# Element work of an attention-and-FFN kernel laid out anew over VectorE, ScalarE and GpSimd

## The chip, the cores and the metric

The kernel runs on one core of one Trainium2 chip. The metric is the device time of one execution in microseconds (us); lower is better. In this document PE is TensorE (matrix multiplies), DVE is VectorE, ACT is ScalarE, POOL is GpSimd and SP is SyncE, which here only starts transfers. PEld is PE's weight load. SBUF is the core's working memory and PSUM the memory that PE writes its results to. All times that are compared come from runs in the same, fast state, with a granted TensorE clock of 0.98 to 1.00.

## The reference, cut to what matters

Four batches, four heads and 1088 tokens of 32 values go through an attention without softmax, and its output (4352 tokens of 128 values) through a feed-forward network (FFN) with 2048 hidden values.

```python
def phi(x):                       # two sketches of 8 values, and all 64 products of them
    a = einsum('rd,bhsd->bhsr', S1, x)
    b = einsum('rd,bhsd->bhsr', S2, x)
    return einsum('bhsi,bhsj->bhsij', a, b).reshape(..., 64)
q_p, k_p = phi(q), phi(k)
kv  = einsum('bhsf,bhsd->bhfd', k_p, v)
z   = sum(k_p, axis=2)
num = einsum('bhsf,bhfd->bhsd', q_p, kv)
den = einsum('bhsf,bhf->bhs',  q_p, z)[..., None] + 1e-06
x   = (num / den)                 # then as 4352 x 128
h   = maximum(x @ w_in, 0)
out = (h * h) @ w_out
```

## The kernel before

The FFN is the spine of the program. Its tokens are cut into 12 chunks: each batch has two of 384 tokens and one of 320. A chunk takes 16 steps, one for each 128 hidden values. A step is one fp16 matmul (`pg`, the first FFN layer), a relu from PSUM to SBUF (`gt`), a square (`g2`), and one fp32 matmul (`po`, the second layer), which the trace records as two instructions. That makes 192 steps, and the attention of later chunks is slipped in between them, because it would otherwise leave PE idle.

A small planner puts every attention task at a step. It looks for the first step after the task's inputs at which its engine has room:

```python
class _Plan:
    LAG = {"PE": 2, "DVE": 1, "ACT": 1, "POOL": 1, "SP": 1}
    def add(self, key, eng, dur, needs, f, *args, not_in=(), first=0, lag=None):
        s = first
        for k in needs:
            s = max(s, self.at[k] + (self.LAG[eng] if lag is None else lag))
        while s < self.n - 1 and (
            (self.load[eng][s] > 0 and self.load[eng][s] + dur > self.cap[eng]) or ...):
            s += 1
        self.fix(key, eng, dur, s, f, *args)
...
P = _Plan(NS + 4, {"PE": 0.95, "DVE": 1.2, "ACT": 0.6, "POOL": 5.0, "SP": 9.0})
```

The k work of a batch n (once per batch, for batches 1 to 3) is planned in this order, and the last chunk of the batch before it was planned ahead of all of it:

```python
def k_tasks(n):
    for g in range(2):
        P.add(("fs", n, g), "DVE", 0.45, [("kf", n)], a_fs, n, g)
    P.at["X"] = P.at["fs", n, 1]
    P.add(("qT", n), "DVE", 1.25, [("fs", n, 0)], a_qT, n, 0, S)      # q of the whole batch
    P.add(("qg", n, 0), "PE", 0.5, ["X", ("qT", n)], a_qg, n, 0)
    for g in range(2):
        P.add(("kp", n, g), "DVE", 1.36, [("fs", n, g)], a_kp2, n, g)  # the 64 products of k
    P.add(("ks1", n), "DVE", 1.15, [("kp", n, 1)], a_ks1, n)           # sums of kp, for z
    P.add(("ks2", n), "DVE", 1.0, [("ks1", n)], a_ks2, n)
    P.add(("kv", n), "PE", 1.4, [("ks2", n), "N"], a_kv9, n)
    ...
```

"N" and "X" stand for two PSUM tiles that tasks share, and so for when they come free. The x work of a chunk divides numerator by denominator and scales the result by a power of two, so that it fits fp16:

```python
def a_rd(b, ch):
    ...
    nc.vector.tensor_scalar(out=de[:, 0:m], in0=_ap(st[b, "dT", ch], 0, 128, 0, [[32, m]]),
                            scalar1=1e-6, scalar2=None, op0=add)       # SBUF to SBUF, 12 values
    nc.vector.reciprocal(rd[:, 0:m], de[:, 0:m])
...
def a_qpn(b, ch, s):                                                   # the 64 products of q
    nc.vector.tensor_tensor(out=qp..., in0=st[b, "sh", ch, s, 0]..., in1=st[b, "sh", ch, s, 1]..., op=mult)
def a_s2(b, ch):                                                       # sm is in PSUM
    nc.vector.tensor_scalar(out=s2..., in0=st[b, "sm", ch]..., scalar1=EXP, scalar2=None, op0=band)
def a_rs(b, ch):                                                       # s2 is in SBUF
    nc.vector.tensor_scalar(out=rs..., in0=st[b, "s2", ch]..., scalar1=EXP, scalar2=None, op0=bxor)
def a_xs(b, ch):
    nc.vector.tensor_tensor(out=st[b, "xT"]..., in0=st[b, "x", ch]..., in1=st[b, "rs", ch]..., op=mult)
def a_beta(b, ch):                                                     # same tile twice
    nc.gpsimd.tensor_tensor(out=bt..., in0=st[b, "s2", ch]..., in1=st[b, "s2", ch]..., op=mult)
```

The relu of every step is on ACT. The square goes to ACT or DVE by a rule that looks at the planned attention work of this step alone, and remembers nothing of the steps before:

```python
def ffn1(i, sq_on_act, cols=None):
    ...
    nc.scalar.activation(gt[:, c0:c1], pg[:, c0:c1], Relu)
    if sq_on_act:
        nc.scalar.activation(g2[:, c0:c1], gt[:, c0:c1], Square)
    else:
        nc.vector.tensor_tensor(out=g2[:, c0:c1], in0=gt[:, c0:c1], in1=gt[:, c0:c1], op=mult)
...
def act_square(i):
    s = max(i - LA, 0)
    return P.load["ACT"][s] + 0.47 + 0.41 < P.load["DVE"][s] + 0.46
```

## Time and profile before

| before | value | from |
|---|---|---|
| time | 203.65 us, median of 3 runs (203.53 to 204.09) | the timed runs |
| span of the profiled run | 201.6 us | the page |
| PE busy | 192.5 us, 95% | the page |
| undisturbed step of 384 tokens, of 320 | 0.807 us, 0.674 us | starts of `pg` in the timeline |
| PE stretching, step 4 to the end of chunk 10 | 8.8 us | worked out, see below |

The page's first part gives busy time, share of the span and number of instructions of each engine. The second line below is its part on the chain of work that ended last, by engine.

```profile
PE 192.5 (95%) x1639; PEld 113.2 (56%) x1639; DVE 159.1 (79%) x369; ACT 149.1 (74%) x346; POOL 24.8 (12%) x86
...
PE 67%; DVE 16%; ACT 10%; issue 3%; DVEq 0%; ACTq 0%
```

PE looks full, at 95%, but a quarter of the chain runs through DVE and ACT. Both are true at once: a matmul that waits for its operand while another is in flight counts as busy. So the busy share does not tell what can be won. I therefore took the starts of successive `pg` matmuls, and compared each step's period with a floor: the period of those steps that hold the same PE matmuls and wait for nothing. Such periods repeat within about 0.01 us. The floor is 0.807 us (or 0.674 us), plus the attention matmuls in the step, above all 0.58 us for `qg` (the sketches of q), 1.29 for `ndn` (numerator and denominator) with `kf` (the sketches of k), about 1.2 for `ndn` with `qg`, 0.14 for `sm` (the sum behind the scale). At a change of chunk the two layers work on different widths, and the floor is 0.781 or 0.701 us. The excess, summed over steps 4 to 175, that is to the end of chunk 10, is 163.9 - 155.1 = 8.8 us. I call it PE stretching. The first four steps, which take 2.55 us in before, are left out.

The groups by form (line, engine, operation, out<-in, partitions x elements, count | busy us, mean ns | idle before, and what ended it) tell who does the element work of before:

```profile
L687 ACT ACTIVATE gt<-pg 128x384 f32<-128x384 f32 x127 | 60.5, 481 | 17.8 <-PE pg L678 16.0 <-DVE g L691 1.1
L691 DVE TENSOR_TENSOR g<-gt 128x384 f32<-128x384 f32 x55 | 30.1, 557 | 18.1 <-ACT gt L687 17.7
L521 DVE TENSOR_TENSOR xT<-x,rs 128x384 f16<-128x384 f32 x6 | 6.4, 1062 | 0.2
L434 DVE TENSOR_TENSOR qp<-sh 128x384 f32<-128x384 f32 x12 | 6.6, 548 | 0.2
L339 DVE TENSOR_TENSOR ks<-kp 128x1024 f32<-128x1024 f32 x3 | 3.7, 1224 | 0.1
```

Two products of the same size, `xT` and `qp`, take 1062 and 548 ns: `xT` runs while POOL computes `bt`, `qp` does not.

The stretching has two forms. The first is in this piece of the timeline of ACT and PE (start us, duration us, engine, line, operation). Relu and square of successive steps are both on ACT, 0.47 and 0.53 us, and `pg` starts every 0.93 us instead of 0.81:

```profile
66.77 0.53 ACT L689 ACTIVATE g<-gt 128x384 f32<-128x384 f32 x1
66.79 0.32 PE L678 MATMUL pg<-xT,w_in 128*128 128x384 f16 x1
67.20 0.47 ACT L687 ACTIVATE gt<-pg 128x384 f32<-128x384 f32 x1
67.70 0.52 ACT L689 ACTIVATE g<-gt 128x384 f32<-128x384 f32 x1
67.72 0.32 PE L678 MATMUL pg<-xT,w_in 128*128 128x384 f16 x1
```

The second form is DVE late around the k work. This is the timeline of DVE in batch 2's k work, with two lines of PE's:

```profile
79.72 1.27 DVE L252 STREAM_TRANSPOSE qT<-qn 128x1088 f32<-128x1088 f32 x1
80.91 1.31 DVE L284 TENSOR_TENSOR kp<-fs 128x1152 f32<-128x1152 f32 x1
81.13 0.56 PE L416 MATMUL qg<-qT,sqn 64*32 64x192 f32 x16 [0.26 <-DVE qT L252]
86.65 1.23 DVE L339 TENSOR_TENSOR ks<-kp 128x1024 f32<-128x1024 f32 x1
87.91 1.15 DVE L350 TENSOR_TENSOR ks<-ks 128x512 f32<-128x512 f32 x2
89.12 0.32 PE L327 MATMUL kvp<-ks,ones 128*32 128x64 f32 x8
```

PE waits for `qT` before it can do `qg`, and a step's square that DVE should do sits behind each of these instructions of 1.2 us and more, which are longer than a whole step.

### The profile page before, as it was taken

What the parts mean: (1) busy time and instruction counts of PE and PEld (TensorE: products, weight loads), DVE (VectorE), ACT (ScalarE), POOL (GpSimd) and SP (SyncE); (2) the same over time, 40 slices, a digit from 0 to 9 for tenths busy, and PEclk for the clock granted to TensorE, in tenths of its full rate; (3) what the DMA queues carried; (4) which work ended last, traced back from release to release, by engine and by line L of the source; (5) the groups of instructions that cost most, each with busy time, mean ns of one, the idle gap of its engine ahead of it and who ended that gap; (6) DMA issues with size and microseconds to landing.
All of it is one profiled execution on the core that took longest, in us unless ns stands there. A gap on an engine that the chain in (4) does not pass through costs nothing.

```text
span 201.6 us, 4402 instructions
## 1 busy us (share of the span) xinstructions
PE 192.5 (95%) x1639; PEld 113.2 (56%) x1639; DVE 159.1 (79%) x369; ACT 149.1 (74%) x346; POOL 24.8 (12%) x86
## 2 busy tenths in 40 slices
PE   7998999999999999999999999999999999999990
PEld 2963755446656455465545555455646555555890
DVE  3866975997888877998899777998799876676750
ACT  3456977997698968975969976976777987766730
POOL 4835132100010100100011000100010110000000
PEclk9999999999999999999999999999999999999997
DMA  6799410200284110020056220020020020010201
GB/s 190 192 312 255 139 23 0 42 0 3 34 208 133 16 16 3 2 42 2 0 126 169 81 32 3 0 42 0 2 44 0 0 36 0 14 25 0 39 3 33
DMA packets 27199, 11.40 MB, mean 57 GB/s; under 512 B 19178, under 2 KB 25770, under 8 KB 27178
## 3 DMA queue, kind: packets, MB, share of 16 engines
q1 hardware_dynamic: 26726, 11.02, 22.4%
q8 instruction: 13, 0.21, 0.5%
q10 hardware_dynamic: 452, 0.10, 0.2%
q14 instruction: 8, 0.07, 0.1%
HBM read 8.78 MB, written 2.23 MB: 55 GB/s over the span
## 4 chain that ended last, share of the span: by engine, by line
PE 67%; DVE 16%; ACT 10%; issue 3%; DVEq 0%; ACTq 0%
PE po L701 38%; PE pg L678 13%; ACT gt L687 6%; PE ndn L447 4%; ACT g L689 3%; DVE sh L425 3%; DVE kp L284 2%; PE warm L822 2%; PE pt L718 2%; DVE xT L521 1%; PE kvp L313 1%; DVE ks L339 1%; PE rep L839 1%; DVE ks L350 1%; PE qg L416 1%
## 5 line engine op out<-in xcount | busy, mean ns | idle before, releaser
L701 PE MATMUL po<-g,w_o 128*128 128x384 f32 (+3 forms) x386 | 144.1, 458 | 0.0
L687 ACT ACTIVATE gt<-pg 128x384 f32<-128x384 f32 (+2 forms) x193 | 87.9, 461 | 30.3 <-PE pg L678 28.4
L701 PEld LDWEIGHTS po<-g,w_o 128*128 128x128 f32 x386 | 66.1, 190 | 37.5 <-issue 26.3
L678 PE MATMUL pg<-xT,w_in 128*128 128x384 f16 (+2 forms) x193 | 61.0, 316 | 1.1 <-ACT gt L687 0.4
L689 ACT ACTIVATE g<-gt 128x384 f32<-128x384 f32 (+1 forms) x114 | 57.4, 504 | 3.6
L691 DVE TENSOR_TENSOR g<-gt 128x384 f32<-128x384 f32 (+2 forms) x79 | 41.3, 534 | 22.4 <-ACT gt L687 21.8
L678 PEld LDWEIGHTS <-w_in 128*128 128x128 f16 x193 | 18.8, 97 | 24.7 <-issue 7.1
L530 POOL TENSOR_TENSOR bt<-s 128x384 f32<-128x384 f32 (+1 forms) x10 | 9.2, 916 | 125.4 <-DVE s L503 125.4
L425 DVE STREAM_SHUFFLE sh<-qg 128x384 f32<-128x384 f32 (+1 forms) x40 | 20.7, 560 | 0.0
L434 DVE TENSOR_TENSOR qp<-sh 128x384 f32<-128x384 f32 (+1 forms) x20 | 10.4, 522 | 0.3
L521 DVE TENSOR_TENSOR xT<-x,rs 128x384 f16<-128x384 f32 (+1 forms) x10 | 9.9, 993 | 0.3
L447 PE MATMUL ndn<-qp,kw 64*32 64x192 f32 (+1 forms) x320 | 9.4, 318 | 0.6 <-DVE qp L434 0.6
L733 POOL COPY br<-beta 32x3 f32<-32x3 f32 x32 | 7.1, 222 | 12.5 <-DVE beta L641 11.3
L447 PEld LDWEIGHTS ndn<-qp,kw 64*32 64x32 f32 x320 | 5.0, 106 | 6.3 <-issue 2.9
L284 DVE TENSOR_TENSOR kp<-fs 128x1152 f32<-128x1152 f32 x6 | 7.9, 1325 | 0.0
L457 DVE STREAM_TRANSPOSE dT<-ndn 128x384 f32<-128x384 f32 (+1 forms) x10 | 5.5, 554 | 2.0 <-PE ndn L447 2.0
L747 DVE SCALAR_TENSOR_TENSOR sc<-po,bt 128x384 f32<-128x384 f32 (+1 forms) x9 | 4.8, 531 | 2.0 <-PE po L701 1.9
L313 PE MATMUL kvp<-kp,vn 128*32 128x64 f32 (+1 forms) x288 | 6.3, 222 | 0.0
L416 PE MATMUL qg<-qT,sqn 64*32 64x192 f32 (+1 forms) x160 | 5.8, 316 | 0.5 <-DVE qT L252 0.5
L313 PEld LDWEIGHTS kvp<-kp,vn 128*32 128x32 f32 (+1 forms) x288 | 4.9, 109 | 2.2 <-issue 1.1
L822 PE MATMUL warm<-zero 128*128 128x512 f16 x13 | 4.8, 529 | 1.2 <-DVE zero L149 1.2
L492 ACT ACTIVATE ax<-x,tiny 128x384 bf16<-128x384 f32 (+1 forms) x10 | 5.8, 579 | 0.0
(115 smaller groups left out, 136.8 us busy)
## 6 DMA issues: line engine op xcount, KB each, us to landing
vn<-in_v_dram SPq DMA_DIRECT2D x32, 64.0 KB, 3.5
kn<-in_k_dram SPq DMA_DIRECT2D x3, 544.0 KB, 11.1
qn<-in_q_dram SPq DMA_DIRECT2D x3, 544.0 KB, 4.1
out_dram<-oT SPq DMA_DIRECT2D x24, 48.0 KB, 1.8
w_in<-in_moe_w_in_dram SPq DMA_DIRECT2D x2, 512.0 KB, 5.3
w_o<-in_moe_w_out_dram SPq DMA_DIRECT2D x2, 512.0 KB, 10.1
out_dram<-oT SPq DMA_DIRECT2D x12, 40.0 KB, 2.5
out_dram<-ob SPq DMA_DIRECT2D x8, 48.0 KB, 1.8
```

Of the source, the lines that this page charges most:

```text
L284: nc.vector.tensor_tensor(out=_ap(st[b, "kp2"], 0, 128, 128 * NT * g, [[64, 2 * NT], [8, 8], [1, 8]]), in0=_ap(fs, 0, 128, 0, [[16, 2 * NT ...
L313: nc.tensor.matmul(st[b, "kvp"][32 * h : 32 * h + 32, 0:64], _ap(vn[b], 0, n, v0 + dv * h, [[1, 32]]), kp[0:n, at[h] : at[h] + 64], start= ...
L425: nc.vector.stream_shuffle(in_=_ap(st[b, "qg", ch], 0, 128, 0, [[512, 2], [1, n]]), out=_ap(t_, 0, 128, 0, [[n, 2], [1, n]]), mask=mask_q[ ...
L434: nc.vector.tensor_tensor(out=qp[:, 0 : 2 * n], in0=st[b, "sh", ch, s, 0][:, 0 : 2 * n], in1=st[b, "sh", ch, s, 1][:, 0 : 2 * n], op=mult,)
L447: nc.tensor.matmul(nd[32 * h : 32 * h + 32, 512 * g + 192 * i : 512 * g + 192 * i + n], st[b, "kw"][64 * g : 64 * g + 64, 128 * i + 32 * h ...
L521: nc.vector.tensor_tensor(out=st[b, "xT"][:, 384 * ch : 384 * ch + n], in0=st[b, "x", ch][:, 0:n], in1=st[b, "rs", ch][:, 0:n], op=mult,)
L530: nc.gpsimd.tensor_tensor(out=bt[:, 0:n], in0=st[b, "s2", ch][:, 0:n], in1=st[b, "s2", ch][:, 0:n], op=mult)
L678: nc.tensor.matmul(pg[:, c0:c1], w_in[:, 128 * c : 128 * c + 128], st[b, "xT"][:, 384 * ch + c0 : 384 * ch + c1],)
L687: nc.scalar.activation(gt[:, c0:c1], pg[:, c0:c1], Relu)
L689: nc.scalar.activation(g2[:, c0:c1], gt[:, c0:c1], Square)
L691: nc.vector.tensor_tensor(out=g2[:, c0:c1], in0=gt[:, c0:c1], in1=gt[:, c0:c1], op=mult)
L701: nc.tensor.matmul(st["po", b, ch][:, c0:c1], w_o[:, 128 * c : 128 * c + 128], g2s[i][1][:, c0:c1], start=first, stop=(c == NFF - 1), skip ...
```

## The change

The change wants to use POOL, busy for only 12%, and to take load from DVE:

1. Products whose operands are both in SBUF go from DVE to POOL: `qp`, `xT`, one of the two `kp` of a batch, and the sums `ks`.
2. `rs` is read from PSUM instead of from `s2` in SBUF, so that this DVE instruction reads no SBUF.
3. The relu of a step may be on DVE, and a square on POOL. A planner, `balance`, chooses for each step, and carries each engine's backlog from step to step.
4. The order in which tasks are planned changes: `kp` ahead of `qT`, `qT` in three pieces, the x work of the last chunk behind the next batch's k work, loads eight steps earlier, output work a step later. POOL's task durations are given as 0.95 to 2.7 us, and PE's are shortened.
5. The last of the nine token tiles of k has only 64 tokens. Its matmuls with v in `kv` now run over 128 rows for batches 1 to 3, and POOL sets the rows of v behind the tokens to zero.

```diff
     def a_kp2(b, g):
-        nc.vector.tensor_tensor(
+        (nc.vector if g == 0 else nc.gpsimd).tensor_tensor(
...
     def a_kv(b, t):                     # t counts the token tiles of k
-        n, v0, dv = (128, 512 * (t // 4) + 32 * (t % 4), 128) if t < 8 else (64, 1024, 32)
+        n = 64 if b == 0 and t == 8 else 128
+        v0, dv = (512 * (t // 4) + 32 * (t % 4), 128) if t < 8 else (1024, 32)
...
     def a_ks1(b):                       # ks2, qpn and xs likewise
-        nc.vector.tensor_tensor(
+        nc.gpsimd.tensor_tensor(
...
     def a_rs(b, ch):
-            out=rs[:, 0:n].bitcast(U32), in0=st[b, "s2", ch][:, 0:n].bitcast(U32),
-            scalar1=EXP, scalar2=None, op0=bxor,
+            out=rs[:, 0:n].bitcast(U32), in0=st[b, "sm", ch][:, 0:n].bitcast(U32),
+            scalar1=EXP, scalar2=EXP, op0=band, op1=bxor,
...
     def ffn1(i, on, cols=None):
-        nc.scalar.activation(gt[:, c0:c1], pg[:, c0:c1], Relu)
-        if sq_on_act:
+        if on[0] == "ACT":
+            nc.scalar.activation(gt[:, c0:c1], pg[:, c0:c1], Relu)
+        else:
+            nc.vector.tensor_scalar(out=gt[:, c0:c1], in0=pg[:, c0:c1], scalar1=0.0, ..., op0=amax)
+        if on[1] == "ACT":
             nc.scalar.activation(g2[:, c0:c1], gt[:, c0:c1], Square)
         else:
-            nc.vector.tensor_tensor(
+            (nc.vector if on[1] == "DVE" else nc.gpsimd).tensor_tensor(
...
-            P.fix(("ob", b, ch), "DVE", 0.56, s0 + 1, f_ob, b, ch)
+            P.fix(("ob", b, ch), "DVE", 0.56, s0 + 2, f_ob, b, ch)
...
     def loads(n):
+        nc.gpsimd.memset(vn[n][64:128, 1024:1152], 0.0)
...
     def k_tasks(n):
-        P.add(("qT", n), "DVE", 1.25, [("fs", n, 0)], a_qT, n, 0, S)
-        P.add(("qg", n, 0), "PE", 0.5, ["X", ("qT", n)], a_qg, n, 0)
         for g in range(2):
-            P.add(("kp", n, g), "DVE", 1.36, [("fs", n, g)], a_kp2, n, g)
+            P.add(("kp", n, g), ("DVE", "POOL")[g], (1.36, 2.7)[g], [("fs", n, g)], a_kp2, n, g)
+        turn_q(n, 0)
+        P.add(("qg", n, 0), "PE", 0.5, ["X", ("qT", n, 0)], a_qg, n, 0)
...
-        P.fix(("ld", n), "SP", 0.0, s0, loads, n)
+        P.fix(("ld", n), "SP", 0.0, max(s0 - 8, 0), loads, n)
...
-    x_tasks(0, 2)
     for n in range(1, B):
         k_tasks(n)
+        x_tasks(n - 1, 2)
+        kv_tasks(n)
         for ch in range(3):
             feature_tasks(n, ch)
-            if ch == 2 and n + 1 < B:
+            if ch < 2:
+                turn_q(n, ch + 1)
+            elif n + 1 < B:
                 turn_k(n + 1)
             nd_tasks(n, ch)
-            x_tasks(n, ch)
+            if ch < 2:
+                x_tasks(n, ch)
+                P.cap["DVE"] = CAP            # 0.99
+    x_tasks(B - 1, 2)
...
-    def act_square(i): ...
+    def balance():
+        load = {e: P.load[e] + [0.0] * 4 for e in ("PE", "ACT", "DVE", "POOL")}
+        late = {e: 0.0 for e in ("ACT", "DVE", "POOL")}
+        for s_ in range(NS - LA):
+            ...
+            for r, q_ in (("ACT", "ACT"), ("DVE", "ACT"), ("ACT", "DVE"), ("ACT", "POOL")):
+                own_ = {e: load[e][s_] for e in late}
+                own_[r] += cost[r]
+                own_[q_] += cost[q_]
+                if q_ == "POOL" and (late[q_] + own_[q_] > 1.0 or end_ >= -1):
+                    continue
+                end = {e: late[e] + own_[e] + 0.3 * load[e][s_ + 1] for e in late}
+                c_ = max(end["ACT"], end["DVE"]) + 0.02 * (q_ == "DVE") + 0.1 * (q_ == "POOL")
+                ...
+            on[s_ + LA] = best[1]
+            for e in late:
+                late[e] = max(0.0, late[e] + best[2][e] - time)
```

More of the change, by code (lines that the diff above doesn't have):

```diff
@@ L281, in a_kp2 @@
         fs = st[b, "fs", g]
-        if g == 0:
+        if (b, "kp2") not in st:
             st[b, "kp2"] = wpool.tile([128, 2 * 128 * NT], F32, tag="kp2", name="kp2")
-        nc.vector.tensor_tensor(
+        (nc.vector if g == 0 else nc.gpsimd).tensor_tensor(
             out=_ap(st[b, "kp2"], 0, 128, 128 * NT * g, [[64, 2 * NT], [8, 8], [1, 8]]),
@@ L349, in a_ks2 @@
             lo, hi = (_ap(ks, 0, 128, o, [[512, 2], [1, w]]) for o in (0, w))
-            nc.vector.tensor_tensor(out=lo, in0=lo, in1=hi, op=add)
+            nc.gpsimd.tensor_tensor(out=lo, in0=lo, in1=hi, op=add)
     def a_kf2(b):
@@ L433, in a_qpn @@
         qp = st[b, "qpn", ch, s] = bpool.tile([128, 384], F32, tag="qp", bufs=4, name="qp")
-        nc.vector.tensor_tensor(
+        nc.gpsimd.tensor_tensor(
             out=qp[:, 0 : 2 * n], in0=st[b, "sh", ch, s, 0][:, 0 : 2 * n],
@@ L520, in a_xs @@
             st[b, "xT"] = bpool.tile([128, SP], F16, tag="xT", name="xT")
-        nc.vector.tensor_tensor(
+        nc.gpsimd.tensor_tensor(
             out=st[b, "xT"][:, 384 * ch : 384 * ch + n],
@@ L667, in a_xd @@
         )
+    DEBUG = False
+    CAP = 0.99
     steps = [(b, ch, c) for b in range(B) for ch in range(3) for c in range(NFF)]
@@ L672, with ffn1 @@
     g2s = {}
-    def ffn1(i, sq_on_act, cols=None):
+    def ffn1(i, on, cols=None):
         b, ch, c = steps[i]
@@ L686, in ffn1 @@
         gt, g2 = g2s[i]
-        nc.scalar.activation(gt[:, c0:c1], pg[:, c0:c1], Relu)
-        if sq_on_act:
+        if on[0] == "ACT":
+            nc.scalar.activation(gt[:, c0:c1], pg[:, c0:c1], Relu)
+        else:
+            nc.vector.tensor_scalar(
+                out=gt[:, c0:c1], in0=pg[:, c0:c1], scalar1=0.0, scalar2=None, op0=amax
+            )
+        if on[1] == "ACT":
             nc.scalar.activation(g2[:, c0:c1], gt[:, c0:c1], Square)
         else:
-            nc.vector.tensor_tensor(
+            (nc.vector if on[1] == "DVE" else nc.gpsimd).tensor_tensor(
                 out=g2[:, c0:c1], in0=gt[:, c0:c1], in1=gt[:, c0:c1], op=mult
@@ L923 @@
         if m < 2:
-            P.fix(("oT", b, ch), "DVE", 0.55, s0 - 1, f_oT, b, ch)
-            P.fix(("ob", b, ch), "DVE", 0.56, s0 + 1, f_ob, b, ch)
-        else:
-            P.fix(("sc", b, ch), "DVE", 0.55, s0 - 1, f_sc, b, ch)
-            P.fix(("sT", b, ch), "DVE", 0.56, s0 + 1, f_sT, b, ch)
+            P.fix(("oT", b, ch), "DVE", 0.55, s0, f_oT, b, ch)
+            P.fix(("ob", b, ch), "DVE", 0.56, s0 + 2, f_ob, b, ch)
+        else:
+            P.fix(("sc", b, ch), "DVE", 0.55, s0, f_sc, b, ch)
+            P.fix(("sT", b, ch), "DVE", 0.56, s0 + 2, f_sT, b, ch)
     def loads(n):
         alloc_loads(n)
+        nc.gpsimd.memset(vn[n][64:128, 1024:1152], 0.0)
         load_qk(kn[n], k, n, 0, S)
@@ L969, in feature_tasks @@
                 P.add(("sh", b, ch, s_, i), "DVE", 0.58, need, a_sh, b, ch, s_, i)
-            P.add(("qpn", b, ch, s_), "DVE", 0.56, [("sh", b, ch, s_, 1)], a_qpn, b, ch, s_)
+            P.add(("qpn", b, ch, s_), "POOL", 0.95, [("sh", b, ch, s_, 1)], a_qpn, b, ch, s_)
         P.at["X"] = P.at["sh", b, ch, 1, 1]
@@ L981, in nd_tasks @@
         if c_ > 0:
-            P.add(("nd", b, ch), "PE", 1.3, need + [("qT", b)] * (b > 0) + ["X"],
+            P.add(("nd", b, ch), "PE", 0.97, need + [("qT", n_, c_)] * (n_ > 0) + ["X"],
                   pair, (a_ndn, (b, ch)), (a_qg, (n_, c_)))
@@ L985, in nd_tasks @@
         elif n_ < B:
-            P.add(("nd", b, ch), "PE", 1.4, need + ["X"] + [("kT", n_, x_) for x_ in range(3)],
+            P.add(("nd", b, ch), "PE", 1.05, need + ["X"] + [("kT", n_, x_) for x_ in range(3)],
                   pair, (a_ndn, (b, ch)), (a_kf2, (n_,)))
@@ L989, in nd_tasks @@
         else:
-            P.add(("nd", b, ch), "PE", 0.83, need, a_ndn, b, ch)
+            P.add(("nd", b, ch), "PE", 0.6, need, a_ndn, b, ch)
     def x_tasks(b, ch):
@@ L998, in x_tasks @@
         P.add(("sum", b, ch), "PE", 0.17, [("ax", b, ch)], a_sum, b, ch)
-        P.add(("s2", b, ch), "DVE", 0.53, [("sum", b, ch)], a_s2, b, ch)
+        P.add(("rs", b, ch), "DVE", 0.53, [("sum", b, ch)], a_rs, b, ch)
+        P.add(("s2", b, ch), "DVE", 0.53, [("rs", b, ch)], a_s2, b, ch, lag=0)
         P.at["N"] = P.at["s2", b, ch]
-        P.add(("rs", b, ch), "DVE", 0.36, [("s2", b, ch)], a_rs, b, ch, lag=0)
-        P.add(("xs", b, ch), "DVE", 0.56, [("rs", b, ch)], a_xs, b, ch, lag=0)
+        P.add(("xs", b, ch), "POOL", 0.95, [("rs", b, ch)], a_xs, b, ch)
         P.add(("bt", b, ch), "POOL", 1.0, [("s2", b, ch)], a_beta, b, ch)
@@ L1011, in k_tasks, with turn_q, kv_tasks @@
         P.at["X"] = P.at["fs", n, 1]
-        P.add(("qT", n), "DVE", 1.25, [("fs", n, 0)], a_qT, n, 0, S)
-        P.add(("qg", n, 0), "PE", 0.5, ["X", ("qT", n)], a_qg, n, 0)
         for g in range(2):
-            P.add(("kp", n, g), "DVE", 1.36, [("fs", n, g)], a_kp2, n, g)
-        P.add(("ks1", n), "DVE", 1.15, [("kp", n, 1)], a_ks1, n)
-        P.add(("ks2", n), "DVE", 1.0, [("ks1", n)], a_ks2, n)
-        P.add(("kv", n), "PE", 1.4, [("ks2", n), "N"], a_kv9, n)
+            P.add(("kp", n, g), ("DVE", "POOL")[g], (1.36, 2.7)[g], [("fs", n, g)], a_kp2, n, g)
+        turn_q(n, 0)
+        P.add(("qg", n, 0), "PE", 0.5, ["X", ("qT", n, 0)], a_qg, n, 0)
+    def turn_q(n, i):
+        c0, c1 = 384 * i, min(384 * i + 384, S)
+        P.add(("qT", n, i), "DVE", 0.55, [("fs", n, 1)], a_qT, n, c0, c1)
+    def kv_tasks(n):
+        P.add(("ks1", n), "POOL", 2.5, [("kp", n, 0), ("kp", n, 1)], a_ks1, n)
+        P.add(("ks2", n), "POOL", 2.0, [("ks1", n)], a_ks2, n)
+        P.add(("kv", n), "PE", 1.15, [("ks2", n), "N"], a_kv9, n)
         P.add(("kvs", n), "ACT", 0.4, [("kv", n)], a_kvs, n)
@@ L1025, in turn_k @@
         s0 = 48 * (n - 1)
-        P.fix(("ld", n), "SP", 0.0, s0, loads, n)
+        P.fix(("ld", n), "SP", 0.0, max(s0 - 8, 0), loads, n)
         for part in range(3):
-            P.add(("kT", n, part), "DVE", (0.71, 0.71, 0.2)[part], [], a_kT, n, part, first=s0 + 6)
+            P.add(("kT", n, part), "DVE", (0.71, 0.71, 0.2)[part], [], a_kT, n, part,
+                  first=max(s0 - 2, 6))
     P.at["X"] = P.at["N"] = -1
@@ L1034 @@
     nd_tasks(0, 2)
-    x_tasks(0, 2)
     for n in range(1, B):
         k_tasks(n)
+        x_tasks(n - 1, 2)
+        kv_tasks(n)
         for ch in range(3):
             feature_tasks(n, ch)
-            if ch == 2 and n + 1 < B:
+            if ch < 2:
+                turn_q(n, ch + 1)
+            elif n + 1 < B:
                 turn_k(n + 1)
             nd_tasks(n, ch)
-            x_tasks(n, ch)
-    def act_square(i):
-        s = max(i - LA, 0)
-        return P.load["ACT"][s] + 0.47 + 0.41 < P.load["DVE"][s] + 0.46
+            if ch < 2:
[5 more added lines that the diff above has]
+        late = {e: 0.0 for e in ("ACT", "DVE", "POOL")}
+        on = {}
+        for s_ in range(NS - LA):
+            w = 0.8 if steps[s_][1] < 2 else 0.667
+            cost = {"ACT": 0.48 * w / 0.8, "DVE": 0.56 * w / 0.8, "POOL": 0.95 * w / 0.8}
+            time = w + load["PE"][s_]
+            end_ = s_ + LA - (NS - NFF)
+            if 0 <= s_ - (NS - NFF) < LAST:
+                time = 0.47
+            best = None
+            for r, q_ in (("ACT", "ACT"), ("DVE", "ACT"), ("ACT", "DVE"), ("ACT", "POOL")):
[6 more added lines that the diff above has]
+                c_ = max(end["ACT"], end["DVE"]) + 0.02 * (q_ == "DVE") + 0.1 * (q_ == "POOL")
+                if best is None or c_ < best[0]:
+                    best = c_, (r, q_), own_
+            on[s_ + LA] = best[1]
+            for e in late:
+                late[e] = max(0.0, late[e] + best[2][e] - time)
+            if DEBUG:
+                print(s_, "%.2f" % time, best[1], {e: ("%.2f" % load[e][s_], "%.2f" % late[e]) for e in late})
+        return on
+    where = balance()
     for cols in ((0, 128), (128, 384)):
-        ffn1(0, False, cols)
+        ffn1(0, ("ACT", "DVE"), cols)
     for i in range(1, LA):
-        ffn1(i, i % 2 == 1)
+        ffn1(i, ("ACT", ("DVE", "ACT")[i % 2]))
     for cols in ((0, 128), (128, 384)):
@@ L1057 @@
         if i + LA < NS:
-            ffn1(i + LA, act_square(i + LA))
+            ffn1(i + LA, where[i + LA])
         if 0 < i < NS - NFF:
```

## The prediction

> **What bounds the kernel now.** The page of before has TensorE (PE) busy 192.5 of 201.6 us (95%), VectorE (DVE) 159.1, ScalarE (ACT) 149.1, GpSimd (POOL) 24.8. PE work is fixed by the change. The timeline shows an undisturbed FFN step of 384 tokens repeating every 0.81 us, of 320 tokens every 0.675 us. From the starts of the first FFN matmul I subtracted, step by step, those periods and the attention matmuls in between (ndn 0.7-0.8 us, kf or qg 0.49, kv about 1.45). What is left over the 12 token chunks (16 steps each) is about 10 us of PE stretching, in chunks 0 to 9; chunks 10 and 11 have almost none. This is all that the change can win: about 193.5 us at the very best. "PE busy" hides it, because waiting matmuls overlap.
>
> Two forms: (a) runs of steps whose relu and square are both on ACT take 0.93 us, not 0.81 (relu 0.47 + square 0.50); (b) DVE late around the k work of a batch (kp 1.33 us, twice, ks 1.22, 0.69 and 0.43) and with xT: the chain of waits runs through DVE at 81-89, 98-104, 126-135 and 145-151 us.
>
> **What the change moves.** From DVE to POOL: 20 qp (10.4 us), 10 xT (9.9), one of two kp per batch (4.0), ks (7.0). rs now reads PSUM: +1.8. The squares leave DVE (79, 41.3 us). Of 189 planned steps 89 are relu+square on ACT, 69 DVE+ACT, 31 ACT+POOL (read from the built order and the planner). Relu on DVE from PSUM should take what s takes from PSUM: 0.55 (384), 0.48 (320). Sums: DVE 159 to about 125 us, ACT 149 to about 135, POOL 25 to about 80.
>
> POOL cost: bt (384) shows 0.93-1.0 us but begins under rs; less that overlap 0.69, and 0.59 for 320: about 1.65 ns per element. Estimate: kp 1.95 us, ks 1.75+0.9+0.5, chain about 5.1 us, against some 9 steps of room before kv. So PE should not wait for ks.
>
> **What gives part back.** The Trainium skill, "SBUF — State Buffer", section "Who interferes with whom", says a DVE instruction with two SBUF inputs or in a two-port mode and a GpSimd instruction block each other whole. This trace agrees: xT takes 1062 ns under bt, where the like product qp takes 548. After, kp on DVE and kp on POOL start together (POOL waits 1.3 us), then de (SBUF to SBUF tensor_scalar, 0.17 us), perhaps the reciprocal rd, and ob sit behind POOL's kp and ks. That delays x, on which ACT waits in order (ax), once per batch: estimated 0.5-2 us of PE for each of three batches. In chunks 0-1 ACT has ten steps of 0.97 us against PE's 0.81 (8.75 us with qg and sum): about 1 us stays.
>
> Sum: 10 us lost now; about 4-5 stay or come new; gain 5-6 us. **Predicted 198.0 us (0.972), range 194.5 to 201.5.** Faster by over 2%: 0.70, within 2%: 0.27, slower: 0.03.
>
> **What would show it.** Groups: relu on DVE near 0.5 us, POOL squares 0.65-0.75; DVE busy about 125. Steps: chunks 3 to 9 mostly 0.81/0.675 with few 0.93. xT and qp never longer on DVE. Wrong on contention if de beside POOL's kp stays at 0.17 us; right if de or rd reads 1-2 us. Chain of waits: less DVE in chunks 5 and 8, what remains near kp, de and ax.
>
> **What would make it wrong.** POOL slower than 1.65 ns per element (then kv and xT wait for POOL, PE stalls of microseconds); reciprocal blocked too, with relus queued behind it; or no blocking of de at all, then 195.

## More of the kernel before

I sorted the excess by its size in a step: "small" is 0.05 to 0.3 us (nearly all of them ACT-paced steps), "big" is 0.3 us or more (mostly waits for DVE or POOL). Before has 4.9 us of small in 31 steps, and 3.8 us of big in 8 steps.

## The result, and the profile after

| | before | after |
|---|---|---|
| median of the fast runs | 203.87 us (203.53 to 204.36, 4 runs) | 195.71 us (195.53 to 196.11, 4 runs) |
| span of the profiled run | 201.6 us | 194.3 us |
| PE stretching, step 4 to the end of chunk 10 | 8.8 us | 1.2 us |
| small / big | 4.9 / 3.8 us | 0.25 / 0.8 us |

The change is faster, at a ratio of 0.9601 (95% interval 0.9573 to 0.9628). Here and below a ratio is the mean time of one kernel's fast runs over the mean of the other's of the same rounds, so it is not quite the ratio of the medians beside it. All results are correct.

The page of after, the same two parts as above:

```profile
PE 186.2 (96%) x1639; PEld 113.2 (58%) x1639; DVE 131.6 (68%) x326; ACT 141.3 (73%) x322; POOL 97.9 (50%) x162
...
PE 88%; DVE 7%; ACT 1%; issue 1%; DVEq 0%
```

PE runs as many matmuls, 1639, and is busy for 6.3 us less: most of that "busy" of before was waiting. The chain is now 88% PE. The stretching falls by 7.5 us (8.77 - 1.23). Another 0.8 us is PE's own work, by point 5 of the change: the step with `kv` takes 2.27 us where nothing waits, against 2.54 us with the matmuls of before, once in each of three batches (see f4 below). Together this is 8.4 us, against 8.2 us between the medians.

The groups of after by form:

```profile
L691 ACT ACTIVATE gt<-pg 128x384 f32<-128x384 f32 x81 | 38.5, 477 | 6.4 <-PE pg L681 5.8 <-POOL g L699 0.3
L693 DVE TENSOR_SCALAR gt<-pg 128x384 f32<-128x384 f32 x46 | 25.5, 554 | 21.3 <-PE pg L681 20.4 <-POOL xT L522 0.9
L699 POOL TENSOR_TENSOR g<-gt 128x384 f32<-128x384 f32 x16 | 13.2, 827 | 31.6 <-ACT gt L691 31.6
L435 POOL TENSOR_TENSOR qp<-sh 128x384 f32<-128x384 f32 x12 | 12.3, 1029 | 3.7 <-DVE sh L426 3.7
L340 POOL TENSOR_TENSOR ks<-kp 128x1024 f32<-128x1024 f32 x3 | 7.1, 2372 | 0.2
L467 DVE TENSOR_SCALAR de<-dT 128x10 f32<-128x10 f32 x4 | 3.6, 896 | 0.1
L467 DVE TENSOR_SCALAR de<-dT 128x12 f32<-128x12 f32 x6 | 1.0, 174 | 0.2
```

Of the relus of 384 tokens 46 are now on DVE, at 554 ns, which is hardly more than ACT's 477. A product that took DVE 548 ns (`qp`) takes POOL 1029 ns, and `ks` takes 2372 ns instead of 1224. POOL can afford it.

A stretch of steady steps of after, from the timeline of PE, DVE and ACT, shows the relu of one step on DVE, between steps that have theirs on ACT, and `pg` every 0.81 us:

```profile
66.70 0.33 PE L681 MATMUL pg<-xT,w_in 128*128 128x384 f16 x1
67.14 0.56 DVE L693 TENSOR_SCALAR gt<-pg 128x384 f32<-128x384 f32 x1 [0.90 <-PE pg L681]
67.51 0.33 PE L681 MATMUL pg<-xT,w_in 128*128 128x384 f16 x1
67.73 0.52 ACT L697 ACTIVATE g<-gt 128x384 f32<-128x384 f32 x1 [0.17 <-DVE gt L693]
68.32 0.33 PE L681 MATMUL pg<-xT,w_in 128*128 128x384 f16 x1
```

What stays is one big wait of 0.81 us, in the k work of batch 1: the step with `kv` takes 3.08 us there, and 2.27 us in the other two batches. The timeline of all engines there:

```profile
33.03 3.12 POOL L284 TENSOR_TENSOR kp<-fs 128x1152 f32<-128x1152 f32 x1 [1.20 <-DVE fs L277]
35.05 1.14 DVE L467 TENSOR_SCALAR de<-dT 128x10 f32<-128x10 f32 x1
36.22 0.22 DVE L471 RECIPROCAL rd<-de 128x10 f32<-128x10 f32 x1
36.23 2.38 POOL L340 TENSOR_TENSOR ks<-kp 128x1024 f32<-128x1024 f32 x1
38.70 2.28 POOL L351 TENSOR_TENSOR ks<-ks 128x512 f32<-128x512 f32 x2
38.73 1.65 DVE L770 TENSOR_TENSOR ob<-oT,br 128x384 f32<-128x384 f32 x1
42.16 0.47 DVE L504 TENSOR_SCALAR s<-sm 128x320 uint32<-128x320 uint32 x1
42.68 1.21 PE L314 MATMUL kvp<-kp,vn 128*32 128x64 f32 x72 [0.74 <-DVE s L504]
```

`de` adds a constant to ten numbers per partition. It takes 1.14 us, and ends within 0.05 us of POOL's `kp` (36.19 against 36.15 us); where no POOL instruction is in its way the same operation on twelve numbers takes 174 ns. The reciprocal behind it takes 0.22 us, but it starts 0.01 us ahead of `ks`, so these lines alone do not tell whether POOL could block it; e6 does. `ob`, a product of two SBUF tiles, takes 1.65 us instead of about 0.55 beside `ks`. The two delays put `s` late, and PE waits for `s` because it frees the PSUM tile that `kvp` wants.

This agrees with the Trainium skill, page "SBUF — State Buffer", section "Who interferes with whom": a DVE instruction with two SBUF inputs, or in one of the two-port modes that `tensor_scalar` can enter, contends with a GpSimd instruction that reads SBUF, whoever issues first holds the shared ports for its whole instruction, and the other "**fully blocks** (not throttle)". The 1062 ns of `xT` in before, and the 1.14 us of `de` and 1.65 us of `ob` in after, look just like that.

### The profile page after: what moved, and what is told of

Same layout as the page of the kernel before. It is cut to its first block, busy times and chain, and to the rows that moved or that the text cites. A ratio compares the mean times of both kernels' runs of the same rounds, so it can differ in the third digit from the quotient of the medians.

```text
span 194.3 us, 4446 instructions
## 1 busy us (share of the span) xinstructions
PE 186.2 (96%) x1639; PEld 113.2 (58%) x1639; DVE 131.6 (68%) x326; ACT 141.3 (73%) x322; POOL 97.9 (50%) x162
## 4 chain that ended last, share of the span: by engine, by line
PE 88%; DVE 7%; ACT 1%; issue 1%; DVEq 0%
PE po L709 54%; PE pg L681 15%; PE ndn L448 4%; PE kvp L314 3%; PE warm L830 2%; PE pt L726 2%; PE qg L417 1%; PE kf L258 1%; PE rep L847 1%; DVE sh L426 1%; PE kvp L328 1%; PE kf L357 1%; PE kvp L576 1%; DVE ob L770 1%; PE sm L498 1%; PE nd L576 1%
## 5 line engine op out<-in xcount | busy, mean ns | idle before, releaser
L697 ACT ACTIVATE g<-gt 128x384 f32<-128x384 f32 (+1 forms) x159 | 79.9, 506 | 21.3 <-DVE gt L693 17.6
L691 ACT ACTIVATE gt<-pg 128x384 f32<-128x384 f32 (+2 forms) x124 | 56.3, 458 | 13.7 <-PE pg L681 13.0
L693 DVE TENSOR_SCALAR gt<-pg 128x384 f32<-128x384 f32 (+1 forms) x69 | 36.7, 533 | 26.5 <-PE pg L681 25.4
L699 POOL TENSOR_TENSOR g<-gt 128x384 f32<-128x384 f32 (+1 forms) x31 | 23.9, 776 | 47.1 <-ACT gt L691 46.8
L435 POOL TENSOR_TENSOR qp<-sh 128x384 f32<-128x384 f32 (+1 forms) x20 | 19.1, 964 | 6.8 <-DVE sh L426 5.1
L284 POOL TENSOR_TENSOR kp<-fs 128x1152 f32<-128x1152 f32 x3 | 9.5, 3169 | 5.3 <-DVE fs L277 5.3
L522 POOL TENSOR_TENSOR xT<-x,rs 128x384 f16<-128x384 f32 (+1 forms) x10 | 9.5, 950 | 1.7 <-DVE rs L513 1.7
L340 POOL TENSOR_TENSOR ks<-kp 128x1024 f32<-128x1024 f32 x3 | 7.1, 2372 | 0.2
L513 DVE TENSOR_SCALAR rs<-sm 128x384 uint32<-128x384 uint32 (+1 forms) x10 | 5.2, 522 | 2.5 <-PE sm L498 2.5
L351 POOL TENSOR_TENSOR ks<-ks 128x512 f32<-128x512 f32 (+1 forms) x6 | 6.2, 1034 | 0.5
```

What stands on the lines that cost most here:

```text
L284: (nc.vector if g == 0 else nc.gpsimd).tensor_tensor(out=_ap(st[b, "kp2"], 0, 128, 128 * NT * g, [[64, 2 * NT], [8, 8], [1, 8]]), in0=_ap( ...
L435: nc.gpsimd.tensor_tensor(out=qp[:, 0 : 2 * n], in0=st[b, "sh", ch, s, 0][:, 0 : 2 * n], in1=st[b, "sh", ch, s, 1][:, 0 : 2 * n], op=mult,)
L522: nc.gpsimd.tensor_tensor(out=st[b, "xT"][:, 384 * ch : 384 * ch + n], in0=st[b, "x", ch][:, 0:n], in1=st[b, "rs", ch][:, 0:n], op=mult,)
L693: nc.vector.tensor_scalar(out=gt[:, c0:c1], in0=pg[:, c0:c1], scalar1=0.0, scalar2=None, op0=amax)
L699: (nc.vector if on[1] == "DVE" else nc.gpsimd).tensor_tensor(out=g2[:, c0:c1], in0=gt[:, c0:c1], in1=gt[:, c0:c1], op=mult)
```

## The experiments

The first reading of the two traces left several explanations standing, because the change does five things at once. My theory at first (T in the expectations) was that the gain needs two halves, the freed DVE and a planner that remembers backlog, that the new order alone gives nothing, and that what remains is blocking between DVE and POOL at `de` and `ob`. Run e4 proved it wrong on the order; f3 and f4 were then made to test the order. The rivals: the order alone does it; moving the products to POOL alone does it; the squares on POOL do it; the choice of the relu's engine does not matter. The expectations shorten some rivals to letters: R3 is the one that e1 tests (the squares on POOL), and R4 the one that e2 tests (the relu's engine).

Twelve kernels ran, on three chips. Ratios are against runs of before in the same rounds (medians of before: 203.88 us with e1, e3, e4, e5; 203.58 with e2, e6, e7, e9; 203.76 with f1 to f4). "Small" and "big" are the us of PE stretching in steps 4 to 175, as defined above, each from the one profiled run.

| kernel | median us | ratio (95% interval) | small | big |
|---|---|---|---|---|
| before | 203.87 | 1 | 4.9 | 3.8 |
| f4: before with the new order of k and x work | 201.66 | 0.990 (0.987 to 0.993) | 5.0 | 1.5 |
| e4: after with all products, squares and relus as before | 200.01 | 0.980 (0.974 to 0.985) | 4.9 | 0.8 |
| e5: after with the old rule for squares | 200.68 | 0.984 (0.977 to 0.991) | 4.7 | 1.4 |
| e3: after with the products on DVE | 200.87 | 0.984 (0.978 to 0.989) | 5.8 | 0.5 |
| f3: after with the old order of k and x work | 203.24 | 0.997 (0.993 to 1.001) | 0.7 | 9.0 |
| after | 195.71 | 0.960 (0.957 to 0.963) | 0.25 | 0.8 |
| e1: after, no squares on POOL | 195.98 | 0.960 (0.954 to 0.966) | 0.8 | 1.0 |
| e2: after, no relu on DVE | 200.44 | 0.986 (0.982 to 0.990) | 0.7 | 4.8 |
| e9: after, `rs` from SBUF | 197.35 | 0.969 (0.968 to 0.971) | 1.1 | 1.4 |
| e6: after without `de` | 195.21 | 0.959 (0.958 to 0.961) | 0.3 | 0 |
| e7: after, both `ob` six steps later | 196.37 | 0.964 (0.962 to 0.965) | 0.8 | 0.6 |
| f1: meant as after with `de` written otherwise; the same program as after | 196.18 | 0.962 (0.959 to 0.965) | 0.25 | 0.8 |
| f2: as f1, first `ob` six steps later | 195.07 | 0.957 (0.955 to 0.960) | 0.25 | 0 |

The gains of f4, e4, e5, e3 and e2 are clear of noise, since their intervals end below 1, but none is clearly above 2%. Not every expectation of the theory held: it missed in e4, f3 and e7; e2 (by 0.4 us) and e9 (1.6 us where at most 0.8 was expected) went further in the expected direction; and f1 turned out void.

### Which parts carry the gain

**e4_order_only: the new order and placements with the element work as before.** All products back on DVE, the old rule for squares, every relu on ACT. What stays of the change is the order of planning, `rs` from PSUM, the times of loads and outputs, PE's planned durations, and point 5, the `kv` over 128 rows.

```diff
-        nc.gpsimd.tensor_tensor(                    # ks1; ks2, qpn, xs and kp g=1 likewise
+        nc.vector.tensor_tensor(
-    CAP = 0.99
+    CAP = 1.2
-    where = balance()
+    def act_square(i):
+        s = max(i - LA, 0)
+        return P.load["ACT"][s] + 0.47 + 0.41 < P.load["DVE"][s] + 0.46
+    where = {i: ("ACT", "ACT" if act_square(i) else "DVE") for i in range(LA, NS)}
```

> As e3, and relu always on ScalarE with the old rule for the square: what is left of the change is the order of the tasks, rs read from PSUM and the split of qT. Theory T: no gain, 202 to 206 us. Rival R1 (order alone): 195 to 199 us.

Measured: 200.01 us, 3.9 us faster than before, though DVE, ACT and POOL keep nearly all of their work. The big waits fall from 3.8 to 0.8 us, the small ones stay (4.9 us). The theory's "no gain" is wrong, and the rival's 195 to 199 us is missed too: what e4 keeps gives nearly half of the gain. How much of that is the order, f4 tells.

**f4_before_new_order: the order of the k and x work alone, put into before.**

```diff
     def k_tasks(n):
-        P.add(("qT", n), "DVE", 1.25, [("fs", n, 0)], a_qT, n, 0, S)
-        P.add(("qg", n, 0), "PE", 0.5, ["X", ("qT", n)], a_qg, n, 0)
         for g in range(2):
             P.add(("kp", n, g), "DVE", 1.36, [("fs", n, g)], a_kp2, n, g)
+        turn_q(n, 0)                                # qT in three pieces
+        P.add(("qg", n, 0), "PE", 0.5, ["X", ("qT", n, 0)], a_qg, n, 0)
...
-    x_tasks(0, 2)
     for n in range(1, B):
         k_tasks(n)
+        x_tasks(n - 1, 2)
+        kv_tasks(n)
```

> The kernel before with nothing changed but the order of the k work (kp ahead of qT, qT in three pieces, the last chunk's x work planned behind the next batch's k work). If this order is what made the 3.9 us of e4: 199.5 to 201 us. If the other small edits of e4 (rs from PSUM ahead of s2, loads and output work at other steps) share in it: 201.5 to 203.9 us.

Measured: 201.66 us, 2.1 us faster than before, so the order by itself is a quarter of the gain. The big waits fall to 1.5 us. The other 1.7 us between f4 and e4 belong to the rest of e4's edits. About half of this is point 5 of the change. In f4 PE waits for nothing in the step with `kv`, which takes 2.54 us in all three batches; in e4 it takes 2.27 us in all three, together 0.8 us less. The 72 matmuls with v take 1.35 us in f4 and 1.21 us in e4 and after:

```profile
86.45 1.35 PE L313 MATMUL kvp<-kp,vn 128*32 128x64 f32 x72
```

Point 5 is the only edit of these matmuls, but no run has it alone. The rest (`rs` from PSUM ahead of `s2`, earlier loads, later outputs, planned durations) I did not separate, and f4 and e4 ran on different chips.

**e5_products_only: products on POOL, but the old rule for squares.** This is after with only the second half of e4's edit.

```diff
-    where = balance()
+    where = {i: ("ACT", "ACT" if act_square(i) else "DVE") for i in range(LA, NS)}   # the old rule
```

> The products on GpSimd and the new order, but relu always on ScalarE and the old rule for the square (74 squares on VectorE, each with two SBUF inputs, none on GpSimd). Theory T: the stalls around kp, ks and xT go, the 0.93 us steps of ScalarE stay, and squares on VectorE are held up by GpSimd (some at 1 us and more instead of 0.56): 198 to 202 us. Rival R2 (the products are all of it): 195 to 197 us.

Measured: 200.68 us, not faster than e4. DVE is freed and nobody uses it: ACT still does all relus, and `pg` still starts every 0.93 us at 66.32, 67.25 and 68.19 us. DVE's 384-token squares in this kernel had 36 us of idle time before them, almost all ended by ACT's relu (before: 18.1 us):

```profile
L699 DVE TENSOR_TENSOR g<-gt 128x384 f32<-128x384 f32 x45 | 25.3, 575 | 36.0 <-ACT gt L691 35.8
```

So the rival "the products alone" falls.

**e3_products_dve: the planner and its choices, but all products on DVE.** This is after with the first half of e4's edit; the tasks are planned on DVE with before's durations.

```diff
-        nc.gpsimd.tensor_tensor(                    # ks1; ks2, qpn, xs and kp g=1 likewise
+        nc.vector.tensor_tensor(
-        P.add(("qpn", b, ch, s), "POOL", 0.95, ...)  # xs, ks1, ks2, kp likewise
+        P.add(("qpn", b, ch, s), "DVE", 0.56, ...)
-    CAP = 0.99
+    CAP = 1.2
```

> The changed kernel with the products (qp, xT, both kp, ks) back on VectorE; its order of tasks and its planner for relu and square stay. Theory T (the gain is PE time no longer lost to late ScalarE and to late VectorE, and needs both halves): the support work again fills VectorE, so only part of the gain is left: 199 to 203 us. Rival R1 (the new order of tasks alone makes the gain): 195 to 198 us. Rival R2 (freeing VectorE of the support products makes all of it): 203 to 206 us, no gain.

Measured: 200.87 us, again not faster than e4, with 5.8 us of small waits. The planner finds DVE full and so puts fewer relus there (51 instead of 69). Neither half gives anything on top of e4, and both together give 4 to 5 us. This is the main finding: POOL's work pays only because the planner spends the room that it makes.

**f3_new_engines_old_order: everything new except the order of the k and x work.**

```diff
         P.at["X"] = P.at["fs", n, 1]
+        P.add(("qT", n), "DVE", 1.25, [("fs", n, 0)], a_qT, n, 0, S)
+        P.add(("qg", n, 0), "PE", 0.5, ["X", ("qT", n)], a_qg, n, 0)
         for g in range(2):
             P.add(("kp", n, g), ("DVE", "POOL")[g], ...)
-        turn_q(n, 0)
-        P.add(("qg", n, 0), "PE", 0.5, ["X", ("qT", n, 0)], a_qg, n, 0)
...
+    x_tasks(0, 2)
     for n in range(1, B):
         k_tasks(n)
-        x_tasks(n - 1, 2)
         kv_tasks(n)
```

> The changed kernel with the order of the k work of before: qT turned in one piece of 1.27 us ahead of kp, the last chunk's x work planned ahead of the next batch's k work. Engines and planner as changed. If the order is needed because VectorE is full (theory T2): with VectorE relieved the old order costs little, 195.7 to 197.5 us. If the order gives its 3.9 us by itself, independent of the engines (R8): 199 us or more.

Measured: 203.24 us, no gain over before at all. The expectation with a relieved VectorE (195.7 to 197.5 us) is missed. The small waits are gone (0.7 us), but the big ones, 9.0 us, are more than twice before's. The timeline of POOL and PE in the k work of batch 2:

```profile
77.34 3.28 POOL L284 TENSOR_TENSOR kp<-fs 128x1152 f32<-128x1152 f32 x1
80.70 2.37 POOL L340 TENSOR_TENSOR ks<-kp 128x1024 f32<-128x1024 f32 x1
82.72 1.21 PE L314 MATMUL kvp<-kp,vn 128*32 128x64 f32 x72
83.03 0.88 POOL L522 TENSOR_TENSOR xT<-x,rs 128x320 f16<-128x320 f32 x1
83.86 2.06 POOL L351 TENSOR_TENSOR ks<-ks 128x512 f32<-128x512 f32 x2
85.97 0.32 PE L328 MATMUL kvp<-ks,ones 128*32 128x64 f32 x8 [1.93 <-POOL ks L351]
87.27 1.49 PE L709 MATMUL po<-g,w_o 128*128 128x384 f32 x2
```

POOL's chain from `kp` to the last `ks` takes 8.6 us here, with an `xT` in its middle. The planner gives a POOL task one step of lag whatever its length, and 5 us of room in each step, so it placed `kv` six steps (about 5 us) after `kp`. PE stands and waits. In after, `kv` lies nine steps behind `kp` in batch 1 and twelve in the other two, because the x work of the last chunk is planned in between and holds PSUM tile "N". The order makes the room that slow POOL needs; nothing in the planner's figures asks for it.

The wait costs twice. After it the `po` pair takes 1.49 us instead of 0.81 for a while: the granted clock falls. The windows of f3 (from:to in us, length, then busy us and instructions of PE, PEld, DVE, ACT and POOL, granted clock, DMA share, GB/s) show it:

```profile
86.20:90.60 4.40, 4.40 (x20) 2.47 (x13) 2.63 (x8) 2.22 (x5) 1.62 (x3) 0.61 0.02 4
90.60:95.00 4.40, 4.40 (x61) 2.49 (x60) 1.98 (x5) 2.03 (x5) 1.58 (x2) 1.00 0.01 2
```

### Which choices of the planner matter

**e1_no_pool_squares: no square on POOL.**

```diff
-            for r, q_ in (("ACT", "ACT"), ("DVE", "ACT"), ("ACT", "DVE"), ("ACT", "POOL")):
+            for r, q_ in (("ACT", "ACT"), ("DVE", "ACT"), ("ACT", "DVE")):
```

> The changed kernel without squares on GpSimd: the planner shares them out between ScalarE (190) and VectorE (89 relus). Theory T: ScalarE and VectorE have room for the 31 squares in most chunks, so little changes: 195.5 to 198 us. Rival R3 (the 31 squares on GpSimd are what relieves ScalarE): 199 us or more, with steps of 0.93 us back.

Measured: 195.98 us, at a ratio of 0.960, the same as after. The 31 squares on POOL are worth nothing that the times resolve (the stretching is 0.8 us higher); the planner puts 89 relus on DVE instead of 69. This rival falls.

**e2_relu_on_act: all relus on ACT; squares may still go to DVE or POOL, by the planner with backlog.**

```diff
-            for r, q_ in (("ACT", "ACT"), ("DVE", "ACT"), ("ACT", "DVE"), ("ACT", "POOL")):
+            for r, q_ in (("ACT", "ACT"), ("ACT", "DVE"), ("ACT", "POOL")):
```

> The changed kernel with every relu on ScalarE (193): the planner relieves ScalarE by squares on VectorE (67, two SBUF inputs) and GpSimd (34) instead of relus on VectorE (one PSUM input). Theory T: the element work is the same, but the squares on VectorE and GpSimd's products block each other: squares on VectorE at 0.7 us and more on average instead of 0.56, GpSimd's products longer too, 197 to 200 us. Rival R4 (any even sharing of the squares and relus does it, no matter which engine reads what): within 0.5 us of the changed kernel.

Measured: 200.44 us, 4.7 us over after. The small waits are nearly as few as in after (0.7 us against 0.25), so what takes those away is the planner with memory on a freed DVE, whichever piece it moves. But the big ones are 4.8 us. A square on DVE reads SBUF twice, and beside POOL's products it now takes 680 ns on average (557 in before), where the relu from PSUM took 554 ns in after:

```profile
L699 DVE TENSOR_TENSOR g<-gt 128x384 f32<-128x384 f32 x43 | 29.1, 680 | 25.4 <-ACT gt L691 25.3
```

PE's waits there end with POOL's `qp` and with `s` on DVE. So this rival falls too: which piece goes to DVE matters. That blocking is what delays these waits fits the durations, but I did not isolate it from the other effects of a different plan.

**e9_rs_sbuf: `rs` from `s2` in SBUF again, after `s2`.**

```diff
-            out=rs..., in0=st[b, "sm", ch]..., scalar1=EXP, scalar2=EXP, op0=band, op1=bxor,
+            out=rs..., in0=st[b, "s2", ch]..., scalar1=EXP, scalar2=None, op0=bxor,
...
-        P.add(("rs", b, ch), "DVE", 0.53, [("sum", b, ch)], a_rs, b, ch)
-        P.add(("s2", b, ch), "DVE", 0.53, [("rs", b, ch)], a_s2, b, ch, lag=0)
+        P.add(("s2", b, ch), "DVE", 0.53, [("sum", b, ch)], a_s2, b, ch)
+        P.add(("rs", b, ch), "DVE", 0.36, [("s2", b, ch)], a_rs, b, ch, lag=0)
```

> The changed kernel with rs computed from s2 in SBUF again (in before 0.36 us) in place of from PSUM (0.55 us). Theory T: rs then is an instruction that GpSimd blocks and that blocks GpSimd: some of the ten rs take 0.7 us or more, xT starts one instruction later, and the time is 0 to 0.8 us longer in spite of less VectorE work. Rival R6 (less work on VectorE counts): 0 to 0.5 us shorter, rs at 0.36 us.

Measured: 197.35 us, 1.6 us slower than after. The shorter instruction is the longer one where POOL is busy: read from SBUF, `rs` of 320 tokens takes 566 ns on average, against about 330 ns undisturbed and 476 ns from PSUM in after. Two of the ten `rs` took over 0.7 us, as expected, but the loss is twice the 0.8 us that was expected at most. `rs`, and with it `xT`, also comes one instruction later, and the two effects are not separated.

```profile
L513 DVE TENSOR_SCALAR rs<-s 128x320 uint32<-128x320 uint32 x4 | 2.3, 566 | 0.1
```

### What remains: `de` and `ob`

**e6_no_de: without `de`.** The reciprocal reads `dT` itself. This drops the guard of 1e-6 against a zero denominator; it is an experiment and not a proposal.

```diff
-        nc.vector.tensor_scalar(out=de..., in0=_ap(st[b, "dT", ch], 0, 128, 0, [[32, m]]), scalar1=1e-6, ...)
-        nc.vector.reciprocal(rd[:, 0:m], de[:, 0:m])
+        nc.vector.reciprocal(rd[:, 0:m], _ap(st[b, "dT", ch], 0, 128, 0, [[32, m]]))
```

> The changed kernel with the add of 1e-6 to the denominators (de, a VectorE instruction from SBUF to SBUF that took 1.14 us beside GpSimd's kp instead of 0.17) left out; the reciprocal reads the denominators themselves. The result is off by about 1e-6 of a denominator, on purpose. Theory T: the three blocked de cost PE time in the first batch only, where the next steps are on a late ScalarE: 0.3 to 1.0 us less than the changed kernel. Rival R5 (blocking on VectorE is hidden everywhere): within 0.2 us.

Measured: 195.21 us, with a ratio of 0.959, which the time alone does not tell from after's 0.960. The big wait is gone from the trace (0.81 to 0). `ob` still takes 1.36 us, so two delays together were needed to reach PE.

The same trace tells more of why `de` is held. The reciprocal now reads `dT` in `de`'s place, in the middle of POOL's `kp`:

```profile
32.29 3.13 POOL L284 TENSOR_TENSOR kp<-fs 128x1152 f32<-128x1152 f32 x1 [1.19 <-DVE fs L277]
34.31 0.22 DVE L466 RECIPROCAL rd<-dT 128x10 f32<-128x10 f32 x1
```

It takes 217 ns in all three batches, where `de` with the same input took 1.14 us. So neither the place, nor the data, nor reading and writing SBUF beside `kp` is what holds `de` (the rival that f1 calls R7); it lies in the instruction itself. The two-port mode fits this, and is not shown by it.

**e7_ob_late: both `ob` six steps later.**

```diff
-            P.fix(("ob", b, ch), "DVE", 0.56, s0 + 2, f_ob, b, ch)
+            P.fix(("ob", b, ch), "DVE", 0.56, s0 + 8, f_ob, b, ch)
```

> The changed kernel with ob (VectorE product of two SBUF tiles, 1.65 us beside GpSimd's ks instead of 0.55, in the steps where PE loses its last microsecond) put six steps later, behind the ks work. Theory T: ob runs at 0.55 us and 0.3 to 1.0 us is won. Rival R5: within 0.2 us.

Measured: 196.37 us, no gain where 0.3 to 1.0 us had been expected. Both `ob` now take 0.55 us and the wait in batch 1 is gone, but a new one comes up at 67 us. The second `ob`'s output transfer now stands ahead of the next batch's loads in SP's queue, `kn` lands late, and DVE waits 3.77 us for it. A relu behind that is late for PE:

```profile
65.50 0.24 DVE L215 STREAM_TRANSPOSE kq<-kn 128x64 f32<-128x64 f32 x1 [3.77 <-DMA kn<-in_k_dram]
...
67.11 0.32 PE L681 MATMUL pg<-xT,w_in 128*128 128x384 f16 x1 [0.47 <-DVE gt L693]
```

**f1_de_one_port: `de` with its output folded,** meant to keep `de` out of the two-port mode and so to test why POOL blocks it. The condition that the expectation takes from the Trainium skill without naming the place is that of the page "VectorE: DVE Perf Modes", section "What auto-detection actually checks": the mode needs outermost sizes of input and output that are both even, or equal.

```diff
-            out=de[:, 0:m], in0=_ap(st[b, "dT", ch], 0, 128, 0, [[32, m]]),
+            out=_ap(de, 0, 128, 0, [[m // j, j], [1, m // j]]),
+            in0=_ap(st[b, "dT", ch], 0, 128, 0, [[32, m]]),
```

> The changed kernel with the same de instruction on the same numbers, only its output pattern folded (3 x 4 or 5 x 2 instead of 12 or 10), so that the outermost sizes of input and output are neither both even nor equal: by the Trainium skill the two-port mode is then not taken. Theory T (de is blocked by GpSimd's kp because it runs in a two-port mode): all ten de at 0.16 to 0.25 us, the stall of 0.66 us at the kv work of the first batch goes, 0.4 to 0.9 us less than the changed kernel's 195.7. Rival R7 (de is held by something else, for instance the data dependence or any SBUF read beside kp): the three de stay at 1.1 us and the time does not move.

Measured: 196.18 us, `de` still 1.14 us. As a test this is void. The built program merged the folded pattern back into one dimension, so that its input and output patterns are those of after; it is a repeat of the changed kernel, and it tells only how well that repeats on another chip (0.962 against 0.960).

**f2_de_one_port_ob_late: as f1, and the `ob` of the first chunk alone six steps later.** Since f1's edit has no effect, this is after with one number changed for one chunk.

```diff
-            P.fix(("ob", b, ch), "DVE", 0.56, s0 + 2, f_ob, b, ch)
+            P.fix(("ob", b, ch), "DVE", 0.56, s0 + (8 if m == 0 else 2), f_ob, b, ch)
```

> As f1, and ob of the first token chunk alone eight steps behind its chunk instead of two, behind the ks work. The earlier try moved both ob, and the second then stood in front of the next batch's loads in the DMA queue. Theory T: ob at 0.55 us, the load not delayed, 194.6 to 195.3 us, no slower than f1. Rival R5 (blocking on VectorE is hidden once de is out): equal to f1 within 0.2 us.

Measured: 195.07 us, the best of all kernels that compute the full reference, at a ratio of 0.957 to before. `de` still takes 1.14 us, the first `ob` 0.55, and no big wait is left. Against f1 of the same rounds that is 0.5% less; the two intervals against before (0.955 to 0.960, and 0.959 to 0.965) just touch, so by time alone this is weak. The trace of each shows what was removed.

## Why the prediction was right

Predicted were 198.0 us, from 194.5 to 201.5, and 195.71 was measured: right in direction and inside the range, with more gain than the middle of it. Point by point:

- **What bounds the kernel, and how much can be won.** PE, with stretching that its busy share hides: about 10 us were predicted, and 8.8 us are found from step 4 on. The two forms were right too, and the experiments take them away one at a time: the order of the k work removes most of the big waits (f4), and the freed DVE with the planner the small ones. That "PE work is fixed by the change" was wrong: point 5 took 0.8 us off `kv`.
- **Durations on DVE and ACT.** The relu on DVE was put at 0.55 and 0.48 us, and took 554 and 490 ns.
- **Where DVE gets blocked.** `de` beside POOL's `kp` was expected at 1 to 2 us and took 1.14, three times; `ob` was named too, and took 1.65 us. The reciprocal, a "perhaps", is not blocked: 217 ns, in e6 even in the middle of `kp`.
- **What this blocking costs** was mis-sized. The prediction has "estimated 0.5-2 us of PE for each of three batches". It was 0.81 us in the first batch and nothing in the other two, where no `ob` follows `de`.
- **The early chunks.** "In chunks 0-1 ... about 1 us stays" was about 0.3 us by the step periods.
- **So the mis-sized term of the sum is "about 4-5 stay or come new".** 1.2 us stayed from step 4 on. The sum by the record is 8.8 lost, less 1.2 that stayed, plus 0.8 of shorter PE work: 8.4 us of gain in place of "5-6". The misses partly cancel, since less was lost than the 10 us of the sum. That is luck.
- **POOL's cost was too low, without harm to PE.** "About 1.65 ns per element" was read from `bt`, whose two inputs are the same operand. Squares, which are alike, took 827 ns (384) and 721 (320), a slope of 1.66 ns, though the 0.65 to 0.75 us that were predicted for them were too low. With two different operands the slope is 2.14 ns (`ks` of 1024 elements 2372 ns, of 512 1274 ns). The chain of `kp` and `ks` took 7.8 us, not "about 5.1": `ks` took 4.7 us in place of 3.15, and POOL's `kp` 3.12 to 3.19 us beside DVE's `kp`, against 2.16 us in the two places where that did not run beside it (f3 and e9). The prediction names this wait of POOL but leaves it out of the chain. POOL was busy for 98 us, not 80; DVE for 131.6, not 125; ACT for 141.3, not 135. "So PE should not wait for ks" came true by the room before `kv`, nine to twelve steps, and not by the estimate; f3 shows what six steps cost.
- **What the prediction left out is the order of planning.** It speaks of work moved between engines. By the runs, the new order is worth 2.1 us (f4), or 3.9 us with the other placements and the shorter `kv` (e4), and without the order of the k and x work the moved work brings nothing (f3, 203.24 us).

Left open: what in `de` is blocked (it is not its place or its data, by e6, but the skill's two-port mode is argued and not shown, since f1 was void); which of e4's other edits give the last 0.9 us between it and f4; and how much of e2's loss is blocking.

## What to carry to other kernels

Measure what can be won by the periods of the repeated step against an undisturbed one with the same matmuls, since a pipelined engine that waits still reads as busy, and look whether the change alters that engine's own work as well. Moving work to an idle engine pays only if the room that it makes is spent, here by a planner that remembers backlog, and only if the slow engine's chain gets its real duration as lead time, here through the order of planning. Beside a busy GpSimd it was better here to give VectorE the work that reads PSUM (e2, e9), even where that instruction alone is slower; neither run isolates the blocking.

## What the Trainium skill lacked or had wrong

- "SBUF — State Buffer", section "Who interferes with whom", names copies, casts and `tensor_scalar` as able to block and be blocked, and `tensor_reduce` as not, but says nothing of the reciprocal. Here an SBUF-to-SBUF reciprocal of ten fp32 values took 217 ns in the middle of POOL's `kp` (e6), while `de`, a `tensor_scalar` of the same values, took 1.14 us there. What the section does state agrees with `xT`, `de` and `ob`; that `de` runs in a two-port mode is not shown.
- "GPSIMD Engine Reference", section 3.1 "Elementwise — side-by-side cycle accounting", gives about 2.6 cycles per element for two inputs, and 4497 ns for 2048 elements, which is 2.2 ns each. The 2.14 ns per element here, with two different operands, agree. It does not tell the case of the same operand as both inputs: 1.66 ns per element, from the 827 and 721 ns of the squares.
- "TensorE: Matmul & The Clock Gate", section "Why this matters for your kernels", advises no PE-idle gaps over about 3 us between bursts, else the clock falls to half. In f3 shorter waits were enough. After one of 1.93 us, in a stretch of 4.2 us (82.0 to 86.2 us) in which PE was busy for 2.27 us, the granted clock was 0.61 over the next 4.4 us. After one of 2.71 us, in a stretch of 4.2 us (127.3 to 131.5 us) with PE busy for 1.49 us, it was 0.50 over the next 3.4 us. (Another section of the page tells of short idle times that make the clock fall, but gives no length for them.)
